# Residual by DMA transposes, a stored instruction order, and shorter runs for the k and v loads in a retention + gMLP kernel

## The chip, the cores and the metric

The kernel runs on one core of one Trainium2 chip. The metric is the device time of one execution in microseconds (us), as the median of several executions. The profile is one execution recorded by the hardware profiler. Its span (first to last instruction) is some 2 us shorter than the time. PE is the matrix engine, PEld its weight loads, DVE the vector engine, ACT the scalar engine, POOL the general engine, and SP the engine that issues nearly all DMAs here ("SPq" in a chain is SP's queue, busy with issuing).

Executions come in states: "slow" when an execution is more than 1.5% above the fastest of the same kernel. The medians in the tables are over all executions, so where one of them was slow, a difference is given here by the means of the fast ones. A ratio is the mean time of one kernel's fast runs over that of the kernel before's fast runs of the same rounds on the same chip, so it isn't quite the ratio of the medians that are quoted.

## The reference, cut to what matters

```python
# q, k, v: [8, 8, 576, 64] float32: batch, heads, sequence, head size
scores = scale * (q @ k.T)                       # per head
ret    = scores * where(rel >= 0, gamma ** rel, 0)
x      = (ret @ v) -> [8, 576, 512]              # heads side by side
h      = gelu(x @ w_in);  u, v = halves of h     # w_in: 512 x 1024
v_n    = layernorm(v) * g_ln
v_s    = einsum('ts,bsd->btd', w_sg, v_n) + b_sg # 576 x 576, along the sequence
out    = x + (u * v_s) @ w_out                   # x is the residual
```

## The kernel before

Two batches make a pair, and a pair has nine tiles of 128 rows of x. It is loaded as four full blocks (256 rows of the sequence of q, k and v) and one half block in the middle, so there are 20 blocks in 4 pairs. Every piece of work is a job with an engine, an estimated length and a due time. A planner inside the kernel simulates the engines and greedily picks the order of the jobs. Jobs on PE come in two tilings: matmuls on the whole 128x128 array (V, U, gate W, output) and 64-row ones on parts of the array (transposes T of q and k, scores S, state Z, retention output O).

```python
    # a load of a full block: one DMA each for q, k, v; runs of two rows = 512 B
    nc.sync.dma_start(f_[:], src[2*p+e, :, r0:r0+256, :].rearrange("h (p s) d -> p h (s d)", s=2))
    ...
    def a_T(b):                      # transposes of q and k: 64x64 each, four parts of the array
        for a in (1, 0):
            for kk in range(KK):
                for s in range(ns):
                    for r in range(2):
                        for c in range(2):
                            nc.tensor.transpose(tpf[C, r, o:o+64], qkb[R, s, a, 2*kk+c, :], ident[R, R])
    ...
    def a_OS(b, g):                  # O, then scores of the next block, drain, then the rest of O
        a_O(b, st.pop((b, "zs")))
        a_S(b + 1, g)
        nc.tensor.drain()
        a_O2(b)
    ...
    def m_O(i):                      # an output tile: residual by identity matmuls, then the product
        for j in range(KK):
            nc.tensor.matmul(o6[...], xTs[p][:, j, r], ident[:]..., start=(j == 0), stop=False)
        for c in range(KK):
            nc.tensor.matmul(op[:], gTs[p][:, c, r], w_out[:, c, :], start=False, stop=(c == KK - 1))
    def m_Oev(i):
        nc.scalar.activation(cur["ob", i][:], cur.pop(("op", i))[:], Act.Copy)
```

Of the kernel before, what the change touches and what calls it, by code (L numbers as in the profile page):

```python
# [19 lines left out]
SWITCH = 95.0  # L20

PR = dict(PB=10200.0, S=4803.0, S2=1401.0, OS=3150.0, Z=1500.0, Z2=2500.0, V=19148.0, V2=2200.0, U=1100.0, W=4554.0, WS=37977.0, slack=129.0, pen=766.0)
# [7 lines left out]
class Job:  # L30
    def __init__(self, eng, dur, due, fn, deps=(), new=None, uses=(), mode=None, nbytes=0, run=0, what=""):
        self.what = what or fn.__code__.co_names[:1]
        self.eng, self.dur, self.due, self.fn = eng, dur, due, fn
        self.deps = [d for d in deps if d is not None]
        self.new = [] if new is None else list(new) if isinstance(new, (list, tuple)) else [new]
        self.mode, self.nbytes, self.run = mode, nbytes, run
        self.start = self.out = None
        self.after = 0.0
        for b in uses:
            b.users.append(self)  # L40
        for b in self.new:
            b.users.append(self)


class Planner:


    def __init__(self, bufs, free, slack=60.0, penalty=500.0, fill=None, fill_until=0.0):
        self.bufs, self.free = bufs, free
        self.slack, self.penalty = slack, penalty  # L50
        self.fill, self.fill_until = fill, fill_until
        self.jobs, self.order = [], {t: [] for t in bufs}
        self.dma_free, self.dmas = 0.0, []
        self.mode = None
# [6 lines left out]
    def ready(self, j):  # L61
        t = self.free[j.eng]
        for d in j.deps:
# [3 lines left out]
            if d.eng == j.eng:  # L67
                lat = j.after if j.eng == "PE" else 60.0
# [13 lines left out]
        if j.eng == "SP" and len(self.dmas) >= 8:  # L82
            t = max(t, self.dmas[-8])
        if j.mode is not None and self.mode is not None and j.mode != self.mode:
            t += SWITCH
        return t

    def place(self, j, t):
        j.start = t
        if j.nbytes:  # L90
            self.free[j.eng] = t + j.dur
            per = (8.0 + 0.0325 * j.run) * j.nbytes / j.run / 16.0
            self.dma_free = max(self.dma_free, t + 1300.0) + per + 100.0
            j.out = self.dma_free + 700.0
            self.dmas.append(j.out)
        else:
            j.out = t + j.dur
            self.free[j.eng] = t + j.dur - OVL[j.eng]
# [4 lines left out]

    def plan(self):
        todo = {e: [] for e in self.free}
# [3 lines left out]
        while any(todo.values()):  # L109
# [15 lines left out]
            if e == "PE" and self.fill and self.free["PE"] < self.fill_until and t0 > self.free["PE"] + 500.0:  # L125
                f = self.fill(int((t0 - self.free["PE"] - 150.0) // 216.0))
# [5 lines left out]
            lim = t0 + self.slack + (SWITCH if e == "PE" else 0.0)  # L132
# [6 lines left out]
        seq = sorted(range(len(done)), key=lambda n: (done[n].start, n))  # L139
        for n in seq:  # L140
            done[n].fn()
        return max(j.out for j in done)


@with_exitstack
def kernel(
# [31 lines left out]
    BUFS = dict(ld=9, qkb=2, vb=3, qkT=2, ret=4, zb=4, xT=2, uT=2, gT=2, vg=3, mv=3, vn=10, ob=3,  # L178
# [14 lines left out]
    NBK = len(RB)  # L193

# [3 lines left out]
    g_col = consts.tile([128, KK], F32, name="g_col")  # L198
    rowg = consts.tile([4, F2], F32, name="rowg")
    rowb = consts.tile([4, S], F32, name="rowb")  # L200
    row4b = consts.tile([4, 2, S], BF, name="row4b")
    row_t = consts.tile([4, F2], F32, name="row_t")
    sel_i = consts.tile([4, 1], I32, name="sel_i")
    sel = consts.tile([4, 3], F32, name="sel")
    warm = consts.tile([128, 512], BF, name="warm")
# [5 lines left out]
    garg = consts.tile([128, 2, NBK * 2, H], F32, name="garg")  # L211
    gqv = consts.tile([128, 2, NBK * 2, H], F32, name="gqv")
# [4 lines left out]
    nc.scalar.dma_start(rowg[:], moe_g_ln.partition_broadcast(4))  # L217
    nc.scalar.dma_start(rowb[:], moe_b_sg.partition_broadcast(4))
    nc.scalar.dma_start(g_col[:], moe_g_ln.rearrange("(c p) -> p c", p=128))
# [6 lines left out]
    make_identity(nc, ident[:])  # L226
    for h in range(H):
        nc.vector.tensor_scalar(garg[:, 0, :, h], srow[:].rearrange("p n s -> p (n s)"), lng[h], lsc,
                                op0=Alu.mult, op1=Alu.add)
    nc.vector.tensor_scalar(garg[:, 1, :, :], garg[:, 0, :, :], -1.0, lsc, op0=Alu.mult, op1=Alu.add)  # L230
    nc.scalar.activation(gqv[:].rearrange("p a m h -> p (a m h)"), garg[:].rearrange("p a m h -> p (a m h)"), Act.Exp)
# [9 lines left out]
    nc.gpsimd.iota(sel_i[:], pattern=[[0, 1]], base=0, channel_multiplier=1)  # L241
    def fill(n):
        bf = Buf("d")

        def f():
            scr = psD.tile([128, 512], F32, name="scr", tag="d")
            for _ in range(n):
                nc.tensor.matmul(scr[:], warm[:, :128], warm[:], start=True, stop=True, skip_group_check=True)  # L248
        return Job("PE", 216.0 * n, 0.0, f, new=bf, mode="F")

    pl = Planner(BUFS, dict(PE=700.0, DVE=2600.0, ACT=2600.0, POOL=2600.0, SP=0.0), slack=PR["slack"], penalty=PR["pen"],
# [3 lines left out]
    HB = [PB, PB, PB / 2, PB, PB]  # L255
    T0 = []
    t = 9000.0
    for n in range(NP * NBK):
        T0.append(t)
        t += HB[n % NBK]  # L260


    wst, jw = {}, {}

    def win_load(half, c):
        bf = Buf("ld")

        def f():
            wst[half, c] = new("ld", [128, 2, F2], F32)
            w4 = moe_w_in.rearrange("(a c h d) f -> a c d h f", a=2, c=2, h=2)  # L270
            for cc in range(2):
                nc.sync.dma_start(wst[half, c][64 * cc:64 * cc + 64],
                                  w4[c, cc, :, :, half * F2:(half + 1) * F2])
        jl = add("SP", 1000.0, 0.0, f, new=bf, nbytes=1 << 19, run=2048)
        eng = "DVE" if c == 0 else "ACT"

        def g():
            src, dst = wst.pop((half, c)), w_in[:, 2 * c:2 * c + 2, half * F2:(half + 1) * F2]
            if eng == "DVE":
                nc.vector.tensor_copy(dst, src[:])  # L280
            else:
                nc.scalar.activation(dst, src[:], Act.Copy)
        jc = add(eng, 690.0 if eng == "DVE" else 1020.0, 0.0, g, deps=[jl], uses=[bf])
        jw[half, c] = jc
        return jl, jc

    def sg_load(j):
        bf, n, k_ = Buf("ld"), min(128, S - 128 * j), ("sg", j)

        def f():  # L290
            wst[k_] = new("ld", [128, S], F32)
            nc.sync.dma_start(wst[k_][:n], moe_w_sg[128 * j:128 * j + n, :])

        def g():
            nc.scalar.activation(wnat[:n, j, 64:64 + S], wst.pop(k_)[:n], Act.Copy)
        jl = add("SP", 500.0, 0.0, f, new=bf, nbytes=n * S * 4, run=2304)
        jc = add("ACT", 645.0, 0.0, g, deps=[jl], uses=[bf])
        return jl, jc

    def wo_load(c):  # L300
        bf, k_ = Buf("ld"), ("wo", c)

        def f():
            wst[k_] = new("ld", [128, 2, F2], F32)
            nc.sync.dma_start(wst[k_][:], moe_w_out.rearrange("(c p) f -> p c f", p=128)[:, c:c + 2, :])
        jl = add("SP", 500.0, 0.0, f, new=bf, nbytes=1 << 19, run=2048)
        js = []
        for r in range(2):
            def g(r=r):
                nc.scalar.mul(w_out[:, c + r, :], wst[k_][:, r, :], g_col[:, c + r:c + r + 1])  # L310
            js.append(add("ACT", 700.0, 0.0, g, deps=[jl], uses=[bf]))
        return jl, js
# [4 lines left out]
    xTs, uTs, gTs = {}, {}, {}  # L317
    cur = {}

    def a_load(b, t):  # L320
# [5 lines left out]
        if ns == 2:  # L326
            e, r0 = ch[0]
            nc.sync.dma_start(f_[:], src[2 * p + e, :, r0:r0 + 256, :].rearrange("h (p s) d -> p h (s d)", s=2))
# [4 lines left out]
    def a_prep(b, t):  # L333
# [3 lines left out]
        src = f_[:, :, :ns * D].rearrange("p h (s d) -> p s h d", s=ns)  # L337
        if t in "qk" and (b, "qkb") not in st:
            st[b, "qkb"] = new("qkb", [128, 2, 2, H, D], BF)
        if t == "k":  # L340
            nc.gpsimd.tensor_copy(st[b, "qkb"][:, :ns, 1], src)  # L341
            return
        if t == "v":
            st[b, "vb"] = new("vb", [128, 2, H, D], BF)
            dst = st[b, "vb"][:, :ns]
        else:
            dst = st[b, "qkb"][:, :ns, 0]
        a = 0 if t == "q" else 1
        for s in range(ns):
            nc.gpsimd.tensor_tensor(dst[:, s], src[:, s],  # L350
                                    gqv[:, a, 2 * n + s, :].unsqueeze(2).to_broadcast([128, H, D]), op=Alu.mult)

    def a_T(b):
# [5 lines left out]
        qkb = st[b, "qkb"]  # L359
        for a in (1, 0):  # L360
            for kk in range(KK):
                for s in range(ns):
                    o = ((a * KK + kk) * ns + s) * 64
                    for r in range(2):
                        for c in range(2):
                            R, C = slice(64 * r, 64 * r + 64), slice(64 * c, 64 * c + 64)
                            nc.tensor.transpose(tpf[C, r, o:o + 64], qkb[R, s, a, 2 * kk + c, :], ident[R, R])  # L367

    def a_Tev(b):
        ns = RB[b % NBK][0]  # L370
        w = 2 * KK * ns * 64
        nc.vector.tensor_copy(st[b, "qkT"][:].rearrange("p c a k t -> p c (a k t)")[:, :, :w],  # L372
                              st.pop((b, "tp"))[:].rearrange("p c a k s t -> p c (a k s t)")[:, :, :w])
# [502 lines left out]
```

## Time and profile before

| | kernel before |
|---|---|
| time, median | 241.68 us (240.2 to 243.03, 3 runs); with the run beside the changed kernel 240.94 us (238.7 to 243.03, 4 runs) |
| span of the profiled run | 239.6 us |
| PE busy | 215.4 us, 90% |
| DVE, ACT, POOL busy | 57%, 56%, 53% |
| time in DMA packets, mean of the 16 DMA engines | 155.3 us |
| transposes of block 5 start on PE | 60.68 us |
| first gate matmul on PE | 61.32 us |
| last matmul starts | 235.4 us |

The lines themselves stand in the prediction below. The page is read from the top: who is busy, then when (the slices), then what the end waited for (the chain), then which group of instructions that is. A high busy share alone doesn't bound the time. The chain does, because it is followed back from the last instruction.

### The profile page before, as it was taken

Reading aid. Unit: us, or ns where it says so; the run is one execution under the profiler, and the core shown is the slowest. Engines: PE = TensorE matmul, PEld = TensorE weight load, DVE = VectorE, ACT = ScalarE, POOL = GpSimd, SP = SyncE. Lnnn points to the kernel's source line nnn. Section 1 sums busy time; section 2 is a strip of 40 time slices with the busy share of each in tenths; the row PEclk is TensorE's granted clock in tenths of the full one; section 3 lists DMA queues with packets and bytes.
Section 4 is the critical chain, followed back from the end, with each engine's and each line's share of the span. In section 5 each row is a group of like instructions: output and inputs, shape, how many; then the busy total and the mean of one; then the engine's idle time right before and its main releaser. Section 6 shows DMA issues by size and latency. Waiting matters only on the chain.

```text
span 239.6 us, 10051 instructions
## 1 busy us (share of the span) xinstructions
PE 215.4 (90%) x4440; PEld 148.0 (62%) x4485; DVE 137.1 (57%) x230; ACT 135.1 (56%) x234; POOL 126.8 (53%) x198
## 2 busy tenths in 40 slices
PE   7975839887989999999999999899999999999993
PEld 2442617654766676677676667566757666667761
DVE  7991626665765745665667466374756555634420
ACT  2027247865656475576645665767473656865422
POOL 8955645499595569772437497906083802221000
PEclk9999989999999999999999999999999999999998
DMA  6999589999899985898564658971110220111324
GB/s 177 251 237 259 138 260 328 290 277 267 176 302 280 310 219 149 244 294 238 149 196 137 193 140 253 298 198 47 48 47 11 80 94 34 59 47 44 131 92 175
DMA packets 70765, 42.92 MB, mean 179 GB/s; under 512 B 14817, under 2 KB 63993, under 8 KB 70721
## 3 DMA queue, kind: packets, MB, share of 16 engines
q1 hardware_dynamic: 70176, 42.26, 63.4%
q8 instruction: 35, 0.57, 1.1%
q10 hardware_dynamic: 544, 0.02, 0.2%
q14 instruction: 10, 0.07, 0.1%
HBM read 32.80 MB, written 9.44 MB: 176 GB/s over the span
## 4 chain that ended last, share of the span: by engine, by line
PE 76%; DMA 13%; issue 4%; ACT 3%; SPq 1%; POOL 1%; ACTq 0%
PE wp L575 17%; PE hu L559 13%; PE op L596 13%; PE hv L517 12%; PE pp L439 7%; DMA ld<-in_q_dram 4%; PE pp L367 4%; PE pp L393 4%; PE op L593 3%; DMA ld<-in_moe_w_out_dram 3%; DMA ld<-in_moe_w_in_dram 3%; PE zp L421 3%; DMA ld<-in_moe_w_sg_dram 2%; ACT xT L506 1%; PE scr L248 1%
## 5 line engine op out<-in xcount | busy, mean ns | idle before, releaser
L403 DVE TENSOR_TENSOR ret<-pp,msk 128x1024 bf16<-128x1024 f32 x32 | 38.9, 1220 | 27.8 <-PE pp L393 27.6
L350 POOL TENSOR_TENSOR qkb<-ld,gqv 128x512 bf16<-128x512 f32 x36 | 37.1, 1051 | 15.6 <-DMA ld<-in_q_dram 12.9
L350 POOL TENSOR_TENSOR vb<-ld,gqv 128x512 bf16<-128x512 f32 x36 | 38.2, 1081 | 5.8 <-DMA ld<-in_v_dram 3.6
L575 PE MATMUL wp<-wT,vn 128*128 128x288 bf16 x256 | 41.2, 286 | 0.0
L582 DVE TENSOR_TENSOR gT<-wp,uT 128x288 bf16<-128x288 f32 x64 | 28.7, 453 | 21.0 <-PE wp L575 20.8
L533 POOL TENSOR_SCALAR mv<-mv 128x2 f32<-128x2 f32 (+1 forms) x20 | 4.5, 226 | 67.5 <-DVE mv L529 48.9
L559 PEld LDWEIGHTS <-w_in 128*128 128x128 bf16 x576 | 34.4, 98 | 6.9 <-issue 0.3
L559 PE MATMUL hu<-xT,w_in 128*128 128x128 bf16 x576 | 38.3, 219 | 0.2 <-issue 0.2
L517 PE MATMUL hv<-w_in,xT 128*128 128x512 bf16 x122 | 35.6, 380 | 2.6 <-ACT xT L506 1.4
L528 DVE BATCH_NORM_STATS2 bst<-vg 128x6 f32<-128x512 f32 x36 | 24.8, 690 | 19.3 <-ACT vg L521 19.3
L596 PE MATMUL op<-w_out,gT 128*128 128x512 bf16 x127 | 33.4, 379 | 0.9
L521 ACT ACTIVATE vg<-hv 128x512 f32<-128x512 f32 x36 | 21.5, 596 | 20.3 <-PE hv L517 18.1
L600 ACT ACTIVATE ob<-op 128x512 f32<-128x512 f32 x36 | 21.4, 595 | 19.4 <-PE op L596 19.4
L372 DVE COPY qkT<-pp 128x2048 bf16<-128x2048 bf16 (+1 forms) x20 | 22.2, 1111 | 15.1 <-PE pp L367 15.1
L565 ACT ACTIVATE uT<-hu 128x512 bf16<-128x512 f32 x36 | 21.5, 596 | 15.6 <-PE hu L559 15.6
L548 ACT ACTIVATE vn<-vg,mv 128x512 bf16<-128x512 f32 x32 | 25.0, 809 | 8.8 <-POOL mv L536 8.7
L506 ACT ACTIVATE xT<-pp 128x512 bf16<-128x512 f32 (+1 forms) x40 | 24.6, 665 | 8.2 <-PE pp L439 8.2
L575 PEld LDWEIGHTS <-vn 128*128 128x128 bf16 x256 | 23.9, 98 | 6.7
L517 PEld LDWEIGHTS <-xT 128*128 128x128 bf16 x144 | 12.6, 98 | 13.1 <-ACT xT L506 2.4
L341 POOL CAST qkb<-ld 128x1024 bf16<-128x1024 f32 (+1 forms) x20 | 19.5, 975 | 0.5 <-DMA ld<-in_k_dram 0.5
L248 PE MATMUL scr<-warm 128*128 128x512 bf16 x61 | 17.6, 436 | 2.2 <-DVE warm L221 1.2
L421 PE MATMUL zp<-vb,qkb 64*64 64x64 bf16 x480 | 13.8, 194 | 6.1 <-ACT zb L427 4.4
(66 smaller groups left out, 263.9 us busy)
## 6 DMA issues: line engine op xcount, KB each, us to landing
out_dram<-ob SPq DMA_DIRECT2D x36, 256.0 KB, 2.7
ld<-in_q_dram SPq DMA_DIRECT2D x16, 512.0 KB, 5.5
ld<-in_k_dram SPq DMA_DIRECT2D x16, 512.0 KB, 6.9
ld<-in_v_dram SPq DMA_DIRECT2D x16, 512.0 KB, 8.1
ld<-in_moe_w_in_dram SPq DMA_DIRECT2D x8, 256.0 KB, 7.0
ld<-in_moe_w_sg_dram SPq DMA_DIRECT2D x4, 288.0 KB
ld<-in_q_dram SPq DMA_DIRECT2D x8, 128.0 KB, 5.1
ld<-in_k_dram SPq DMA_DIRECT2D x8, 128.0 KB, 3.6
```

The lines of the kernel that those rows point to most:

```text
L350: nc.gpsimd.tensor_tensor(dst[:, s], src[:, s], gqv[:, a, 2 * n + s, :].unsqueeze(2).to_broadcast([128, H, D]), op=Alu.mult)
L372: nc.vector.tensor_copy(st[b, "qkT"][:].rearrange("p c a k t -> p c (a k t)")[:, :, :w], st.pop((b, "tp"))[:].rearrange("p c a k s t -> p ...
L403: nc.vector.tensor_tensor(ret[:].rearrange("p r (k t) -> p (r k) t", k=2), sc[:].rearrange("p r (k t) -> p (r k) t", k=2), msk2[:].rearran ...
L506: nc.scalar.activation(dst, src, Act.Copy)
L517: nc.tensor.matmul(hv[:], xTs[p][:, kk, 128 * m:128 * m + 128], w_in[:, kk, F2:], start=(kk == 0), stop=(kk == KK - 1))
L521: nc.scalar.activation(vgs[i][:], cur.pop(("hv", i))[:], Act.Gelu_apprx_tanh)
L528: nc.vector.bn_stats(bst[:], vgs[i][:])
L548: nc.scalar.activation(vn[:], vg[:], Act.Identity, scale=mv[:, s, 2:3], bias=mv[:, s, 3:4])
L559: nc.tensor.matmul(hu[:, c, :], w_in[:, kk, 128 * c:128 * c + 128], xTs[p][:, kk, 128 * m:128 * m + 128], start=(kk == 0), stop=(kk == KK ...
L575: nc.tensor.matmul(ps[:], vns[t0 + j][e][:, 128 * c:128 * c + 128], wT[e][j][:, half * HS:(half + 1) * HS], start=(j == 0), stop=(j == SB ...
L582: nc.vector.tensor_tensor(gTs[p][:, c, col:col + HS], cur.pop(("wp", b, c, half))[:], uTs[p][:, c, col:col + HS], op=Alu.mult)
L596: nc.tensor.matmul(op[:], gTs[p][:, c, r], w_out[:, c, :], start=False, stop=(c == KK - 1), skip_group_check=True)
```

## The change

The intent is to take work and waits off PE, and to bring the start forward. The parts:

- The residual of pairs 1 to 3 leaves PE: a DMA transposes x back into rows, and the DVE adds it as it empties the accumulator.
- The planner follows a stored order (searched for beforehand) and no longer plans greedily. Its model also counts a fetch of instructions for each 256 rows of PE, and different switches between tilings. Within PE, the drain ahead of the second part of O is replaced by another job and a semaphore.
- The q and k transposes are joined in twos (64x128), 576 instead of 1152. U jobs take two tiles, so 512 of its matmuls of 128 columns become 256 of 256.
- k and v of a full block are loaded in two DMAs of 256 B runs each. q stays in one DMA of 512 B runs. There are twelve load buffers instead of nine, weights come in fewer DMAs, the small rows for g and b are made on PE and ACT instead of by DMA copies, and block 0's q and k are prepared on DVE and ACT.

```diff
@@ a load of a full block
-            nc.sync.dma_start(f_[:], src[2 * p + e, :, r0:r0 + 256, :].rearrange("h (p s) d -> p h (s d)", s=2))
+            rows = src[2 * p + e, :, r0:r0 + 256, :].rearrange("h (p s) d -> p h s d", s=2)
+            if t == "q":
+                nc.sync.dma_start(f_[:], rows)
+            else:
+                for s in range(2):
+                    nc.sync.dma_start(f_[:, :, s * D:s * D + D], rows[:, :, s])
@@ transposes of q and k
-                        for c in range(2):
-                            nc.tensor.transpose(tpf[C, r, o:o + 64], qkb[R, s, a, 2 * kk + c, :], ident[R, R])
+                        ins = nc.tensor.transpose(tpf[:, r, o:o + 64], qkb[R, a, kk, s].rearrange("p c d -> p (c d)"), ident[R, R])
@@ the second part of O
-            a_S(b + 1, g)
-            nc.tensor.drain()
+        on = pend.pop(b)
+        if on is None:
+            nc.tensor.drain()
+        elif on:
+            nc.tensor.wait_ge(swap, on)      # an early matmul of the job in between has counted it up
@@ the output
+    XP = 1
+        if p < XP:                           # identity matmuls for pair 0 alone
...
+    def m_X(i):
+        cur["xr", i] = new("xr", [128, KK, 128], BF)
+        nc.sync.dma_start_transpose(cur["xr", i][:], xTs[p][:, m].rearrange("p j r -> p (j r)"))
     def m_Oev(i):
+        if i // NT < XP:
+            ins = nc.scalar.activation(ob[:], op[:], Act.Copy)
+        else:
+            ins = nc.vector.tensor_tensor(ob[:], op[:], cur.pop(("xr", i))[:].rearrange("p j r -> p (j r)"), op=Alu.add)
@@ the order
+ORDER = ( '0 f9 1 6 81 2 111 83 7 f11 ...' )    # 34 lines; job numbers, fN is filler matmuls
     def plan(self):
+        if ORDER:
+            return self.follow(ORDER)
... (joined weight loads, rows of g and b, gate written over u, fused POOL work: cut)
```

## The prediction

> **What bounds the kernel now.** I read the page from the top: busy time per engine, then the slices.
>
> ```profile
> PE 215.4 (90%) x4440; PEld 148.0 (62%) x4485; DVE 137.1 (57%) x230; ACT 135.1 (56%) x234; POOL 126.8 (53%) x198
> ## 2 busy tenths in 40 slices
> PE   7975839887989999999999999899999999999993
> ...
> PEclk9999989999999999999999999999999999999998
> DMA  6999589999899985898564658971110220111324
> ```
>
> The reader is to see two stages. From slice 11 (60 us) to slice 38 the matrix engine (PE) is 90% busy or more at full clock, while DMA runs dry after slice 28. In the first ten slices PE has holes and DMA is at eight or nine tenths: the start waits for loads. A busy PE may still be a slow PE, so the next view is the chain that ended last.
>
> ```profile
> PE 76%; DMA 13%; issue 4%; ACT 3%; SPq 1%; POOL 1%; ACTq 0%
> PE wp L575 17%; PE hu L559 13%; PE op L596 13%; PE hv L517 12%; PE pp L439 7%; DMA ld<-in_q_dram 4%; PE pp L367 4%; PE pp L393 4%; PE op L593 3%; DMA ld<-in_moe_w_out_dram 3%; DMA ld<-in_moe_w_in_dram 3%; PE zp L421 3%; DMA ld<-in_moe_w_sg_dram 2%; ACT xT L506 1%; PE scr L248 1%
> ```
>
> The path is matmuls, with 13% of DMA, all of it before 45 us when the chain is read in order of time. The stage table confirms it (columns: us, busy us of PE, weight loads, DVE, ACT, POOL, then clock, DMA share, GB/s):
>
> ```profile
> 0.00:20.00 20.00, 17.22 (x219) 8.26 (x223) 16.93 (x31) 4.62 (x7) 14.07 (x31) 1.00 0.99 230
> 20.00:40.00 20.00, 12.35 (x307) 8.63 (x309) 7.91 (x14) 10.90 (x19) 11.06 (x14) 0.91 0.89 230
> 40.00:60.00 20.00, 16.61 (x427) 11.75 (x430) 12.53 (x21) 12.37 (x23) 15.69 (x22) 1.00 1.03 286
> 60.00:110.00 50.00, 47.61 (x1151) 34.19 (x1159) 31.00 (x50) 31.61 (x57) 34.44 (x49) 1.00 0.94 249
> 110.00:160.00 50.00, 47.51 (x1078) 33.48 (x1086) 29.83 (x48) 30.68 (x55) 29.44 (x43) 1.00 0.71 202
> 160.00:203.00 43.00, 41.79 (x937) 29.63 (x947) 25.11 (x43) 25.66 (x46) 18.14 (x29) 1.00 0.13 46
> ```
>
> In the chain in order of time the same U job (16 matmuls) of successive pairs of batches starts at 129.80 and 180.62: one pair takes 50.8 us. Steady savings must come out of that period. The groups that matter:
>
> ```profile
> L559 PE MATMUL hu<-xT,w_in 128*128 128x128 bf16 x576 | 38.3, 219 | 0.2 <-issue 0.2
> L593 PE MATMUL op<-ident,xT 128*128 128x128 bf16 x144 | 13.9, 219 | 0.0
> L582 DVE TENSOR_TENSOR gT<-wp,uT 128x288 bf16<-128x288 f32 x64 | 28.7, 453 | 21.0 <-PE wp L575 20.8
> L403 DVE TENSOR_TENSOR ret<-pp,msk 128x1024 bf16<-128x1024 f32 x32 | 38.9, 1220 | 27.8 <-PE pp L393 27.6
> L367 PE MATMUL pp<-ident,qkb 64*64 64x64 bf16 x1152 | 13.5, 194 | 3.4 <-POOL qkb L341 2.2 <-issue 1.1
> ```
>
> The 219 ns of L559 is latency; start to start the 16 matmuls of a job take 0.89 us, 56 ns each. Costs on PE below are start to start, from the timeline.
>
> [...] 56 ns at 128, 216 ns at 512 columns. [...] going from 128x128 matmuls to 64x64 ones costs 0.093 us beyond streaming, back 0.12 us. [...] 256 B packets took 19.4 ns in the mean (12288 of them), 512 B packets 30.7 ns (49152), so half the bytes cost 63% of the time. [...]
>
> **The change part by part.**
>
> Residual. In pairs 1 to 3 the four identity matmuls (L593) ahead of each output job go: 27 jobs x 4 x 56 ns = 6.1 us of PE, all in the saturated stage, so all on the path. In exchange there are 27 DMA transposes of 128 KB, and 27 output evacuations go from ACT (595 ns) to DVE, as an add. From 453 ns at 288 elements and 1220 ns at 1024, a PSUM read on DVE costs 153 + 1.042 n ns, so 0.69 us at 512: 18.5 us more DVE, 16.1 us less ACT. DVE in a steady pair: 31.0 us per 50 now; plus 9 x 0.69 in a shorter 47 us gives about 36, or 77%. It stays under PE. A transpose at ordinary packet cost is an estimated 512 x 19.4 / 16 = 0.6 us of the engines, 17 us in all, where DMA has room.
>
> U jobs. 512 of the 576 matmuls become 256 of 256 columns: a pair of tiles from 2 x 16 x 55.8 = 1786 ns to 16 x 109.2 = 1747 ns. Sixteen pairs: 0.6 us.
>
> Drains. Before the second part of O the old kernel drains PE after the S job. In the PE timeline the first matmul after it starts 0.32 to 0.34 us after the last of S (15 times between 60 and 203 us). The new order puts another job between and waits for a semaphore of an early matmul of it. I count 18 x 0.30 = 5.4 us.
>
> Order. In the instruction order the switches between large and 64-row jobs fall from 53 to 41 each way: 12 x (0.093 + 0.12) = 2.6 us less. But the q/k transposes, halved from 1152 to 576 of 64x128 tiles, are now a third tiling: borders between them and the other small jobs go from 16 to 30, each now a switch. At some 0.1 us each (my choice, from the other switches) that gives back 3.0 us. Streaming stays: 32 matmuls on two tiles against 64 on four.
>
> Instruction fetch. PE rows fall from 8972 to 6990, mostly from transposes and U. Between 60 and 203 us five stalls inside small-matmul jobs, right behind a 16 KB instruction packet, cost 3.4 us; one of 1.43 us comes earlier. I count 2 us saved.
>
> Steady sum: 6.1 + 0.6 + 5.4 + 2.6 - 3.0 + 2.0 = 13.7 us.
>
> Start. Moving k and v in 256 B runs turns 32768 packets into 65536: (65536 x 19.4 - 32768 x 30.7) / 16 = 16.6 us more of each engine over the whole run, and about 6.4 us in the first five blocks (10 loads of 512 KB x 0.52, and a rest for block five). Against it, weights load in fewer DMAs, the small row copies through DMA vanish, w_out moves behind block five's q and k, and twelve buffers instead of nine let loads run ahead. Before, block 4's transposes start at 50.7 us, though its loads sum to 38.6 us of packets, some 43 us with start and landing: 7 us were lost to queue waits. After: q 7.9, k and v 17.4, half block 3.7, w_in 6.2, w_sg 4.0, sum 39.2, landed at 43.5, transposes at 45; block 5 at about 54.5. Up to block 5's transposes PE had done some 28 us of work by 60.7 us (32.7 lost); by the new order it will have done 30 us by 54.5 (24.5 lost). That is 8 us if the queue never waits; I take 6.
>
> Total 13.7 + 6 = 19.7, so 241.7 - 19.7 = 222 us. The old tail of 4 us stays.
>
> **The rivals.** A: the loads decide. Every full block costs 7 us of DMA instead of 5.9, and PE waits longer for blocks 4 to 6. For it: DMA share is near 1 up to 80 us. Against: after the weights a block needs 7 us and PE about 11 (50.8 / 4.5). If the start gains nothing: 228 us; if it loses 4 us: 232. B: the transposes become the new wait. They stand in the same queue as loads of up to 512 KB, behind stores that wait for their data (the queue's waits for ACT ob were 89 us), with three buffers; a late one holds DVE, which now also frees the score and gate buffers in order. At 0.3 us per output: 8 us back, 230 us. For it: DVE at 77%. Against: DMA shares of 0.71 and 0.13 in that stage. C: the order fits better than I count, few waits left and cheap transposes: 15 us steady plus 9 at the start plus the 3 us of the third tiling, 214 us.
>
> **Range and chances.** Residual and drains are firm, 11.5 us; taken alone they are nearly 5%. Start and waits spread by 8 us each way, more upwards. Prediction 222 us, range 213 to 231. Faster by over 2% means below 236.8: 0.95; within 2%: 0.04; slower: 0.01.
>
> **What would show it.** Right: no identity group beyond 36 matmuls; PE period per pair near 47.5 us; block 5's transposes near 54 us; the gap ahead of O's second part under 0.1 us; 256 B packets near 77800 at about 19 ns; DVE add near 0.69 us and DVE near 150 us. Wrong: PE idle after 60 us released by DVE or by a transpose (B), PE holes before 70 us released by k or v loads (A), or borders of the transposes far from 0.1 us. A period above 49 us would refute the steady sum; first gate matmuls after 58 us would refute the start.

In the trace of the kernel before, from 62 us on, matmuls of 128 columns start every 55.9 ns in the mean, and those of 512 columns every 216 ns (median). The 55.8 and 109.2 ns of the U term (128 and 256 columns) were calculated; for 256 columns a straight line through 56 and 216 ns gives 109.3 as an estimate, and the changed kernel's trace has 109.6 in the mean. That a transpose costs ordinary packets was the assumption; the kernel before has no transpose, and the changed kernel's took 21.4 ns a packet. "Streaming stays" was an expectation: a T job takes 0.71 us on the timeline of the kernel before (64 matmuls from 60.68 us) and 0.64 joined (32 from 67.42 us).

## The result

The changed kernel takes 227.26 us (226.66 to 229.07, 4 runs), against 240.94 us of the kernel before in the same rounds. The ratio is 0.9484 (95% interval 0.9404 to 0.9564). The result is correct and the profiled run is a fast one. So it is faster by over 2%, as predicted, inside the range, and 5.3 us above the predicted 222 us.

Busy time per engine and three rows of the slices, of the changed kernel:

```profile
PE 205.5 (91%) x3514; PEld 138.0 (61%) x3514; DVE 147.8 (66%) x266; ACT 123.3 (55%) x214; POOL 114.2 (51%) x157
## 2 busy tenths in 40 slices
PE   7987599793999999999999689999999999999991
PEclk9999979998599999999999999999999999999999
DMA  6999999989999998989999999999896154344664
```

PE lost ten us of work, but its share of the span hardly rose. DMA is now at eight or nine tenths almost without a break up to slice 30, where before it was at four to six tenths in slices 20 to 24 and ran dry from slice 28 on. And PE has holes where before it had none: slice 10 (3 tenths, with the clock at half in slice 11), and slice 23. The chain that ended last says the same:

```profile
PE 64%; DMA 14%; SPq 8%; POOL 5%; DVE 3%; issue 2%; ACT 1%; POOLq 0%; DVEq 0%
```

It was 76% PE before. DMA transfers, their issue and the POOL work behind them now make 27% of the path. In stages (columns: window, us, then busy us of PE, weight loads, DVE, ACT, POOL, then clock, DMA share, GB/s):

```profile
20.00:40.00 20.00, 16.78 (x351) 11.54 (x345) 12.12 (x22) 15.81 (x30) 13.52 (x18) 0.91 1.10 270
40.00:60.00 20.00, 14.94 (x281) 10.83 (x274) 10.34 (x19) 10.72 (x20) 12.51 (x13) 0.87 0.95 229
60.00:110.00 50.00, 50.00 (x954) 34.87 (x953) 31.03 (x51) 33.58 (x60) 31.92 (x38) 0.99 1.02 232
110.00:160.00 50.00, 47.02 (x919) 31.97 (x918) 36.50 (x59) 28.67 (x52) 31.49 (x41) 1.00 1.15 224
160.00:203.00 43.00, 42.79 (x685) 28.70 (x683) 32.04 (x57) 21.76 (x38) 15.62 (x24) 1.00 0.56 122
```

The DMA share from 60 to 160 us rose from 0.94 and 0.71 to 1.02 and 1.15. (The share is summed from the packets' own times, which overlap a little, so it passes 1 here.) At the holes, the timeline of PE reads (start, us, engine, line, operation, count, and in brackets the idle time before it and what ended it):

```profile
51.02 0.62 PE L586 MATMUL pp<-ret,vb 64*64 64x128 bf16 x32
55.12 1.03 PE L501 MATMUL pp<-ident,qkb 64*128 64x64 bf16 x32 [3.48 <-POOL qkb L455]
...
56.87 1.14 PE L719 MATMUL wp<-wT,vn 128*128 128x288 bf16 x4
...
125.00 0.64 PE L501 MATMUL pp<-ident,qkb 64*128 64x64 bf16 x32 [0.74 <-POOL qkb L455]
126.85 0.44 PE L565 MATMUL zp<-vb,qkb 64*64 64x64 bf16 x16 [1.22 <-POOL vb L461]
```

L455 is POOL's cast of k, which itself waits for the load of k. In the chain, the k load issued at 48.02 us is on the path for 5.88 us, then POOL, then these transposes of block 5. After the idle 3.48 us PE runs at half clock: 15 gate matmuls take 3.71 us of the chain, where ones at full clock take 1.84. The clock's records have half clock from 54.63 to 61.46 us. The clock falls 3.0 us into the gap; in e8 below it is at half behind gaps of 2.75 and 2.40 us as well. So in this execution one late load cost PE twice: the wait, and about 2.9 us at half clock (worked out under e1 below). The fourth execution was granted a clock of 0.991 where this one had 0.977, and it took 227.78 us all the same. So the loss doesn't need the half clock.

Two groups (columns: line, engine, operation, tiles, shapes, count, busy us, mean ns, idle before):

```profile
L762 DVE TENSOR_TENSOR ob<-op,xr 128x512 f32<-128x512 f32 x27 | 18.5, 690 | 8.6 <-PE op L746 8.4
L741 PE MATMUL op<-ident,xT 128*128 128x128 bf16 x36 | 3.5, 219 | 0.0
```

The residual moved as intended: 36 identity matmuls are left of 144, and 27 adds on the DVE take 690 ns each.

### The profile page after: what moved, and what is told of

Same layout as the page of the kernel before. It is cut to its first block, busy times and chain, and to the rows that moved or that the text cites. A ratio compares the mean times of both kernels' runs of the same rounds, so it can differ in the third digit from the quotient of the medians.

```text
span 225.0 us, 8170 instructions
## 1 busy us (share of the span) xinstructions
PE 205.5 (91%) x3514; PEld 138.0 (61%) x3514; DVE 147.8 (66%) x266; ACT 123.3 (55%) x214; POOL 114.2 (51%) x157
## 4 chain that ended last, share of the span: by engine, by line
PE 64%; DMA 14%; SPq 8%; POOL 5%; DVE 3%; issue 2%; ACT 1%; POOLq 0%; DVEq 0%
PE wp L719 16%; PE op L746 12%; PE hu L700 11%; PE hv L653 11%; DMA ld<-in_k_dram 5%; SPq L433 5%; PE pp L586 5%; PE pp L501 3%; PE pp L533 3%; DMA ld<-in_v_dram 2%; PE zp L565 2%; DMA ld<-in_q_dram 2%; DMA wst<-in_moe_w_sg_dram 2%; POOL vb L461 2%; SPq L436 2%
## 5 line engine op out<-in xcount | busy, mean ns | idle before, releaser
L461 POOL TENSOR_TENSOR qkb<-ld,gqv 128x1024 bf16<-128x1024 f32 (+1 forms) x19 | 32.7, 1723 | 24.9 <-DMA ld<-in_q_dram 8.2
L729 DVE TENSOR_TENSOR uT<-wp,uT 128x288 bf16<-128x288 f32 x64 | 28.4, 451 | 22.8 <-PE wp L719 21.5
L461 POOL TENSOR_TENSOR vb<-ld,gqv 128x1024 bf16<-128x1024 f32 (+1 forms) x20 | 34.7, 1733 | 11.2 <-DMA ld<-in_v_dram 9.4
L700 PE MATMUL hu<-xT,w_in 128*128 128x256 bf16 (+1 forms) x320 | 38.2, 266 | 1.0 <-ACT vg L660 1.0
L653 PE MATMUL hv<-w_in,xT 128*128 128x512 bf16 x144 | 37.9, 390 | 0.7 <-ACT xT L642 0.7
L746 PE MATMUL op<-w_out,uT 128*128 128x512 bf16 x144 | 35.8, 380 | 0.0
L700 PEld LDWEIGHTS <-w_in 128*128 128x128 bf16 x320 | 28.2, 99 | 8.7 <-issue 1.6
L688 ACT ACTIVATE vn<-vg,mv 128x512 bf16<-128x512 f32 x32 | 25.1, 810 | 10.7 <-POOL mv L676 10.6
L660 ACT ACTIVATE vg<-hv 128x512 f32<-128x512 f32 x36 | 21.4, 595 | 15.1 <-PE hv L653 8.3
L762 DVE TENSOR_TENSOR ob<-op,xr 128x512 f32<-128x512 f32 x27 | 18.5, 690 | 8.6 <-PE op L746 8.4
L455 POOL CAST qkb<-ld 128x1024 bf16<-128x1024 f32 (+1 forms) x19 | 18.0, 947 | 11.3 <-DMA ld<-in_k_dram 11.3
L574 ACT ACTIVATE zb<-zp 128x256 bf16<-128x256 f32 x32 | 12.2, 381 | 16.0 <-PE zp L565 15.9
L746 PEld LDWEIGHTS <-uT 128*128 128x128 bf16 x144 | 13.0, 98 | 12.3 <-DVE uT L729 0.4
```

Source lines behind the costliest of these rows:

```text
L461: eng.tensor_tensor(dst, src, g.unsqueeze(3).to_broadcast(list(src.shape)), op=Alu.mult)
L653: ins = nc.tensor.matmul(hv[:], xTs[p][:, m, kk, :], w_in[:, kk, F2:], start=(kk == 0), stop=(kk == KK - 1))
L660: unfence(nc.scalar.activation(vgs[i][:], cur.pop(("hv", i))[:], Act.Gelu_apprx_tanh), ("V", i))
L688: nc.scalar.activation(vn[:], vg[:], Act.Identity, scale=mv[:, s, 2:3], bias=mv[:, s, 3:4])
L700: ins = nc.tensor.matmul(hu[:, n, :], w_in[:, kk, 128 * c:128 * c + 128], xTs[p][:, m:m + w, kk, :], start=(kk == 0), stop=(kk == KK - 1), ...
L729: ins = nc.vector.tensor_tensor(uTs[p][:, c, col:col + HS], cur.pop(("wp", b, c, half))[:], uTs[p][:, c, col:col + HS], op=Alu.mult)
```

## The experiments

All twelve kernels gave correct results. The time of the kernel before in the three sets was 240.96, 239.42 and 240.54 us. "The changed kernel with 512 B runs" below means the first experiment's.

| run | kernel | time, us (range) | ratio to before (95%) |
|---|---|---|---|
| | changed kernel | 227.26 (226.66 to 229.07) | 0.9484 (0.9404 to 0.9564) |
| e1_runs512 | changed, k and v in one DMA of 512 B runs | 214.68 (213.87 to 215.26) | 0.8935 (0.8861 to 0.9008) |
| e2_greedy | changed, stored order emptied | 256.00 (254.78 to 257.03) | 1.0655 (1.0562 to 1.0748) |
| e3_resid_pe | changed, residual on PE | 230.07 (228.77 to 233.72) | 0.9560 (0.9464 to 0.9655) |
| e4_drain | changed, with drains | 231.31 (229.96 to 234.40) | 0.9624 (0.9476 to 0.9772) |
| e5_before256 | before, k and v in 256 B runs | 252.80 (251.84 to 253.15) | 1.0559 (1.0517 to 1.0602) |
| e6_two512 | changed, two DMAs, 512 B runs | 213.56 (212.70 to 214.09) | 0.8920 (0.8875 to 0.8964) |
| e7_512_pe | e1, residual on PE | 219.43 (218.75 to 219.97, and one of 515.22) | 0.9161 (0.9116 to 0.9207) |
| e8_512_t64 | e1, 64x64 transposes | 228.32 (225.10 to 233.58) | 0.9468 (0.9382 to 0.9553) |
| e9_512_greedy | e1, stored order emptied | 241.56 (241.03 to 242.08) | 1.0101 (1.0022 to 1.0180) |
| e11_512_shift64 | e1, 64 empty rows ahead on PE | 214.78 (213.86 to 216.24) | 0.8977 (0.8923 to 0.9031) |
| e12_two512_tail | e6, last two residuals on PE | 213.66 (212.55 to 214.23) | 0.8922 (0.8871 to 0.8974) |
| e13_512_drain | e1, with drains | 218.53 (217.42 to 220.47) | 0.9136 (0.9077 to 0.9196) |

### The loads: four runs

The theory was that the 256 B runs of k and v are a loss that the rest of the change pays for. The rival was that the two DMAs let the work on k and v start earlier, or at least cost nothing.

e1_runs512:

```diff
-            if t == "q":
+            if t in "qkv":
                 nc.sync.dma_start(f_[:], rows)
```

> Undoes one part alone: k and v again one DMA a block with runs of 512 bytes; every engine's order is as in the changed kernel. Theory (the loads in 256 B runs are what the gain was lost to): 32768 packets of 30.8 ns in place of 65536 of 21.4 ns free 24.6 us of each DMA engine; the wait for block 5's k (PE idle 3.5 us before 55 us, then half clock, some 3 us) and the PE holes of 112 to 128 us (3.5 us) shrink or go: 218 to 221 us, and the DMA share falls well below 0.9. Rival (the order was made for these loads, or their time is hidden beside PE): within 1% of 227 us.

Measured: 214.68 us, 12.6 us less than the changed kernel, more than expected. The chain that ended last is now nearly all PE:

```profile
PE 88%; issue 3%; DMA 3%; DVE 2%; SPq 1%; DVEq 0%; POOL 0%; ACTq 0%; POOLq 0%
```

The PE order is the same in both, so their times can be compared job by job. The transposes of block 5 start at 49.70 us against 55.12 (5.4 us). Those of block 6 start at 59.08 against 67.42 (8.3 us), and between the two lies the half clock. From there to block 12 nothing more is lost (112.21 against 120.55, again 8.3 us). Block 14's start at 126.86 against 138.48 (11.6 us). So 5.4 us are lost in the start, 2.9 to the half clock behind the hole, and 3.3 between 121 and 139 us, where the waits for k and v shown above lie. The stages of this run:

```profile
40.00:60.00 20.00, 19.84 (x425) 14.21 (x424) 15.04 (x27) 14.66 (x27) 16.74 (x16) 1.00 1.02 266
60.00:110.00 50.00, 49.43 (x962) 35.65 (x966) 33.05 (x53) 34.99 (x63) 32.15 (x42) 1.00 1.05 270
110.00:160.00 50.00, 49.42 (x950) 34.33 (x958) 37.94 (x64) 31.52 (x56) 34.42 (x43) 1.00 0.93 196
```

PE has no hole in the stretch from 40 to 60 us and runs at full clock there, and DMA's share falls under 1 from 110 us.

e6_two512 keeps two DMAs but gives each four heads in 512 B runs:

```diff
-                    nc.sync.dma_start(f_[:, :, s * D:s * D + D], rows[:, :, s])
+                    nc.sync.dma_start(f_[:, 4 * s:4 * s + 4, :], rows[:, 4 * s:4 * s + 4])
```

> The changed kernel with k and v in two DMAs a block still, but each of four heads with 512 B runs. It tells the size of the packets from the number of DMAs. Packet size is the cost: 214 to 217 us, as with one DMA of 512 B runs (214.7). Number of DMAs is the cost (32 more issues of some 0.7 to 1.4 us on the queue's engine): 222 to 227 us.

(The issue time expected there compares with the changed kernel's trace: issuing one k or v load kept SP busy for a median of 0.96 us.)

Measured: 213.56 us, ratio 0.892 against 0.8935 of e1, just below the range expected if the packet size is the cost. The number of DMAs costs nothing that can be seen. The packet size is the whole cost, within that.

e5_before256 puts the same loads alone into the kernel before:

```diff
-            nc.sync.dma_start(f_[:], src[2 * p + e, :, r0:r0 + 256, :].rearrange("h (p s) d -> p h (s d)", s=2))
+            rows = src[2 * p + e, :, r0:r0 + 256, :].rearrange("h (p s) d -> p h s d", s=2)
+            if t == "q":
+                nc.sync.dma_start(f_[:], rows)
+            else:
+                for s in range(2):
+                    nc.sync.dma_start(f_[:, :, s * D:s * D + D], rows[:, :, s])
```

> The kernel before with one part of the change alone: k and v of a full block in two DMAs of 256 B runs, nothing else. Theory (the runs cost engine time, 16.6 us of each engine over the run by the packet records, and the kernel before has slack for only a part of it): the start loses 5 to 6 us and the stretch from 60 to 110 us, at a DMA share of 0.94, a few more: 246 to 254 us, with k and v loads as releasers. Rival (the 12.6 us that they cost in the changed kernel come from its order, which has no slack for them): 240 to 244 us.

Measured: 252.80 us, 13.4 us over the kernel before in the same rounds, at the upper end of the theory; the rival falls. The cost doesn't hang on the new order. But the theory named k and v loads as what PE would wait for, and the largest wait isn't one of them. The largest piece is one hole of PE in the timeline, which the kernel before doesn't have:

```profile
100.12 1.04 PE L522 MATMUL hv<-w_in,xT 128*128 128x512 bf16 x4
107.34 1.87 PE L564 MATMUL hu<-xT,w_in 128*128 128x128 bf16 x16 [6.18 <-ACT ob L605]
```

PE waits for an accumulator that ACT is to empty into an output buffer. That the output buffer was not free because its store stands in the same queue behind the loads is my reading of this line. No run took it apart.

The sizes, from the packet records. 256 B packets took 21.4 ns in the mean in the changed kernel and 512 B packets 30.8 ns. The time in packets per DMA engine was 155.3 us before and 174.0 with the 256 B runs alone. It was 206.6 in the changed kernel and 185.1 with 512 B runs. So the shorter runs cost 18.7 and 21.5 us of every DMA engine. Up to 60 us the four kernels are alike, at 58.4, 57.7, 62.1 and 61.8 us: the engines have no room there, and what is added can only come later.

### The order: two runs

e2_greedy and e9_512_greedy empty the stored order, so that the kernel's own greedy planner runs, with its new model and its new jobs:

```diff
-ORDER = ( '0 f9 1 6 81 2 111 ...' )
+ORDER = ""
```

> Undoes the annealed order alone: the stored order is emptied, so the planner's own greedy choice orders all jobs; all jobs, transposes and loads are as in the changed kernel. If the stored order carries the steady saving (fewer switches, no waits for buffers): 233 to 238 us, with more switches of tiling and PE idle. If the saving comes from the jobs alone (residual off PE, no drains): within 1.5% of 227 us.

Measured: 256.00 us, 28.7 us more than the changed kernel and more than the kernel before. That is outside both expectations.

> The changed kernel with 512 B runs for k and v and the stored order emptied, so that the kernel's own greedy planner orders the jobs. Theory (the order itself is the largest part of the gain, whatever the loads: it was searched over a model that counts waits for buffers, switches and one instruction fetch per 256 rows of PE): 236 to 246 us, with PE busy below 88%. Rival (the greedy order lost 28.7 us with the 256 B runs because it has no slack for these loads): 222 to 230 us.

Measured: 241.56 us, 26.9 us more than e1. The theory holds (PE is busy 88%, at the edge of what it said): against this greedy order, the stored one is worth the same with either loads. The chain of e9:

```profile
PE 60%; DVE 11%; ACT 8%; DMA 5%; POOL 5%; SPq 4%; issue 4%; ACTq 0%; POOLq 0%; DVEq 0%
```

DVE, ACT and POOL stand on the path with 24%, where in e1 PE has 88% of it. With this greedy order, all other parts of the change together bring nothing over the kernel before, which was greedy too. (The greedy planner's due times are those stored beside the order. Whether another set would do better was not tried, so how much of the 27 us is the order and how much a planner with unsuited settings is not shown.) All other runs keep the stored order, which was made for the changed kernel's own jobs. So what they put back is measured in an order that may not suit it.

### The residual: two runs

e3_resid_pe and e7_512_pe put the residual of all pairs back on PE:

```diff
-    XP = 1
+    XP = 4
...
+                        if p >= 1:
+                            add("SP", 0.0, due - 6000.0, lambda: None)   # keeps the numbers of the stored order
```

> Undoes the transposes alone: the residual of all pairs by identity matmuls on PE and evacuated by ACT, in the same order. Theory of the prediction: PE gets 27 x 4 x 56 ns = 6.1 us back, so about 232 to 233 us if nothing waits for transposes. Rival (transposes took 17 us of full DMA engines and held the loads, and the last ones hold the end by 1 us): 227 to 230 us, since the loads' waits shrink by what the transposes took.

Measured: 230.07 us. Its three fast executions have a mean of 229.6 us against 227.6 of the changed kernel, 2.1 us more, and the intervals of the two ratios overlap. The theory's 232 to 233 us fails, the rival's range holds. Its profile fell in a slow execution, so no times are read from it.

> The changed kernel with 512 B runs for k and v, and the residual of all pairs on PE by identity matmuls, as in the kernel before. Without the 256 B runs PE is at 99% from 60 to 195 us, so 27 x 4 matmuls of 56 ns should count in full: 214.7 + 6.1 = 220 to 221 us, less up to 1 us of a shorter tail. Rival (transposes give back about half on the DMA queue whatever the loads, as the 2.8 us with 256 B runs suggest): 216.5 to 218 us.

Measured: 219.2 us in the mean of the three fast executions, 4.6 us more than e1, and 5.7 more than e6, which ran in the same rounds. That lies between the two expectations, nearer to the first. Taking 6.1 us off PE saves some 4.6 to 5.7 us where DMA has some room (a share of 0.93 from 110 to 160 us in e1) and about 2 where it has none (1.15 in the changed kernel). (One of the four executions, the profiled one, took 515.22 us. The median in the table still counts it; see the last section.)

### The drains: two runs

e4_drain and e13_512_drain put a drain ahead of the wait:

```diff
         elif on:
+            nc.tensor.drain()
             nc.tensor.wait_ge(swap, on)
```

> Puts one suspected saving back: a drain of PE before the second part of each O job, all else as in the changed kernel. The prediction counted 18 x 0.30 = 5.4 us for the drains' going. If they cost that: 231 to 233 us. If a drain there is mostly hidden by the switches and semaphore waits that stand there anyway: 227 to 229 us.

Measured: 231.31 us. One of the four executions was slow; the fast ones are 3.3 us above the changed kernel in the mean, with intervals that overlap.

> The changed kernel with 512 B runs for k and v, and a drain of PE ahead of every second part of O, in addition to the semaphore. Prediction's term: 18 x 0.30 = 5.4 us, 220 us. With the 256 B runs it was 4.05 us; if the loads hid a part of it there, 219.5 to 220.5 us here. Rival (a drain behind another job than S costs less than the 0.3 us seen before, and 4 us is its whole worth): 218 to 219.2 us.

Measured: 218.53 us, 3.85 us more than e1, and 3.75 more than e11, which turned out to be a repeat of e1 (see below), in the same rounds. The rival holds: 4 us is the whole worth. In the PE timeline the first matmul behind a drain starts 0.26 to 0.30 us late, as before the change. Without a drain that gap isn't zero everywhere: about 0.02 us behind a Z job but 0.105 us behind joined transposes, because that border is now a switch of tiling (in e8 below, where it is none, the gap is 0.006 us).

### The joined transposes and the instruction fetch: two runs

e8_512_t64 undoes the joining:

```diff
-                        ins = nc.tensor.transpose(tpf[:, r, o:o + 64], qkb[R, a, kk, s].rearrange("p c d -> p (c d)"), ident[R, R])
+                        for c in range(2):
+                            ins = nc.tensor.transpose(tpf[64 * c:64 * c + 64, r, o:o + 64], qkb[R, a, kk, s, c], ident[R, R])
```

> The changed kernel with 512 B runs for k and v, and the q and k transposes as 1152 of 64x64 in place of 576 of 64x128. Theory of the prediction (the joined form is a third tiling, 30 more borders at some 0.1 us = 3.0 us, while the streaming is the same): 64x64 saves 3 us and loses 1 to 2 us to the fetch of 1150 more PE rows: 212.5 to 214.5 us. Rival (the joined form pays for itself by fewer rows and fewer fetch stalls): 216 to 218 us.

Measured: 228.32 us. Its two fast executions have a mean of 226.5 us, some 12 us above e1: the wrong way for the theory and far beyond the rival. The borders did get cheaper (O to T 0.014 us instead of 0.13, T to O 0.006 instead of 0.105). But PE stops at places where it waits for nothing that the profile shows:

```profile
50.24 0.72 PE L502 MATMUL pp<-ident,qkb 64*64 64x64 bf16 x64
...
54.56 0.37 PE L587 MATMUL pp<-qkT,zb 64*64 64x128 bf16 x5 [3.55 <-issue]
...
92.28 0.43 PE L587 MATMUL pp<-qkT,zb 64*64 64x128 bf16 x8 [2.75 <-issue]
...
173.69 0.40 PE L720 MATMUL wp<-wT,vn 128*128 128x288 bf16 x1 [2.40 <-issue]
```

Inside each of these three stops a packet of 16 KB of the instruction queue starts (at 52.00, 89.60 and 171.33 us, taking 1.0 to 1.2 us each). The run has 32 such packets against 27 in e1. The traces' counts go together with PE's rows: the kernel before has 4440 matmuls and 4485 weight loads and 35 such packets, 255 rows a packet; the changed kernel has 3514 of each and 27, 260 rows a packet; e8 has 4090 of each and 32, 256 rows a packet. From these I estimate some 256 rows of PE a packet. And each of the three stops shows the same sign in the records: the next instruction packet starts 3.5 to 3.9 us after the first, and between the two PE started only 24, 12 and 6 weight loads, where 4090 / 32 = 128 is the run's mean between two packets. My reading is that PE had used up what was fetched; no record shows that directly. All three come within 3 us behind a T job. A full T job now has 128 rows, weight loads and transposes, in 0.72 us on the timeline; the joined form has 64 rows in 0.64. After 30 us, gaps of PE of over 1 us sum to 11.1 us in this run, and e1 has none. Each of the three stops also brings half clock (6.83 us from 53.97, 6.83 from 91.52 and 3.41 from 173.44). The profile fell in a slow execution (233.58 us at a clock of 0.962), so this overstates the fast runs, and only the kind of stop is taken from it. The fast execution of 225.10 us had a clock of 0.992, no lower than e1's 0.990, and was still over 10 us slower, so the half clock isn't the main part.

e11_512_shift64 asks whether the stored order depends on where the borders between these packets fall:

```diff
+    for _ in range(64):
+        nc.tensor.nop(nofuse=True)
```

> The changed kernel with 512 B runs for k and v, and 64 rows that do nothing ahead of everything on PE, where PE waits for the first memset anyway. [...] Theory (the stored order puts the fetch borders where PE has other waits or slow rows, and this is why 64x64 transposes, which shift all borders and shorten the time of 256 rows, lost 13.6 us): 216 to 220 us, with stalls of over 0.9 us in other places than in the run with 512 B runs alone. Rival (borders do not matter, only the number of rows does): 213.5 to 215 us.

Measured: 214.78 us against 214.68. But this run is void as a test. That the empty rows would shift all later ones was taken for granted in the expectation. Counting the weight loads that PE had started at each instruction packet gives the same places in both runs (1798 and 1799, 2149 and 2149, 3418 and 3418 at the fourteenth, seventeenth and last packet). A shift of 64 rows, half of them weight loads, would have moved these by 32. So these counts show no shift, the run is a repeat of e1, and all that it shows is that e1's median repeats within 0.1 us. (The ratios to the kernel before, 0.8935 and 0.8977, differ by 1 us, so comparisons between sets of rounds are good to about that.)

So two readings stay open. Either the joined form helps because the dense 64-row jobs have fewer rows, or the stored order was fitted to the places of the fetches and any shift would cost. That PE ran out of instructions in e8 is what its slow profile points to; whether this makes up the 12 us of the fast runs, and which of the two makes the joined form free of it, is not shown.

### A last version

e12_two512_tail takes e6 and has the last two output tiles add their residual on PE:

```diff
+    PEX = set(range(NT)) | {N - 2, N - 1}
-        if p < XP:
+        if i in PEX:
```

> A version that should beat all others: two DMAs of four heads with 512 B runs for k and v, and the last two output tiles with their residual on PE and their evacuation on ACT, as pair 0 has it, so that the end does not wait for the last two transposes (the last DVE adds waited 1.5 us for them with 512 B runs). Theory: PE gains 8 matmuls of 56 ns = 0.45 us, the end loses 1.5 us of waiting: 212 to 213 us against 213.6. Rival (the last store and not the transposes sets the end): 213.5 to 214.5 us.

Measured: 213.66 us against 213.56 of e6. No gain; the time is in the rival's range. In the profiled runs the tail after the last matmul's start did get shorter, from 5.1 to 4.1 us; in the medians this isn't seen. That the last store sets the end is argued, not shown. The best version is the changed kernel with 512 B runs for k and v, in one DMA or two: 11% faster than the kernel before.

## Why the prediction was right or wrong

The class and the range were right. The point was 5.3 us too low, and the parts were further off than the sum. Cut at block 5's transposes, the start saved 5.6 us (60.68 to 55.12; 6 were predicted) and the rest of the span 9.0 us (178.9 to 169.9; 13.7 predicted). In e1 the same cut gives 11.0 and 15.0 us. So the missing part is in the steady sum, and it is missing because of the loads. That the total stayed in the range is in part luck: the 256 B runs cost 12.6 us, of which the sum had 6.4, while the order and the joined transposes brought more than was counted.

**Residual, 6.1 us.** The mechanism was right (36 identity matmuls left, 690 ns per add as worked out, DVE at 147.8 us against the 150 predicted). The size was about 2 us in the kernel as it is and 4.6 to 5.7 us with 512 B runs. The prediction gave the transposes "room" on the DMA engines; that was the mis-sized term. The packets alone say so: 27 x 512 packets x 21.4 ns (the mean of all 256 B packets) / 16 = 18.5 us of each engine. With the transposes taken out, the sum of all packet times falls by more, from 206.6 to 174.5 us in e3 and from 185.1 to 155.2 in e7 (both profiles are of slow executions). The rest is in the other packets, which took longer beside them: those of 4 B took 10 ns in the mean without transposes and 35 and 43 ns with them.

**U jobs, 0.6 us.** Eight matmuls of 256 columns take 0.87 us in the chain, 109 ns each, as predicted. No run tested the term by itself.

**Drains, 5.4 us.** They measured about 3.3 and 3.85 us. The 0.3 us per drain was right. What was missed is that the gap doesn't vanish behind joined transposes (0.105 us). The check "under 0.1 us" held behind Z and failed there.

**Order, 2.6 us, third tiling, -3.0 us, and instruction fetch, 2.0 us.** This was the weakest part. Counting switches gave 2.6 us for the order; emptying it cost 27 to 29. That is not a like for like measure of the old order, but the greedy planner was the old way too. The borders of the third tiling were sized well (0.105 to 0.133 us each). But the joined form as a whole was counted as a loss of 3 us and a part of the 2 us of fetch, while undoing it cost some 12 us. The step that failed is "I count 2 us saved": it added up stalls that the old kernel had, where the question was how many the new order would have without the joining. That these 12 us are fetch stalls is likely from e8's profile and not shown. (PE's rows fell to 7028 and not to 6990.)

**Start, 6 us.** The checks came out well: transposes of block 5 at 55.12 us (predicted "near 54"), first gate matmul at 47.72 (before 58). The estimate of 6.4 us for the 256 B runs up to block 5 is met by 5.4 us in e1. What was missed is the hole itself, 3.48 us behind a load of k, and the half clock after it. The hole is the prediction's own sign that rival A is right ("PE holes before 70 us released by k or v loads").

**Rival A, the loads decide.** It gave 228 us if the start gains nothing, and the result was 227.26. The start did gain, but PE did wait for k and v there and later, as A has it. The argument against A was the step of the prediction that failed: "after the weights a block needs 7 us and PE about 11". It counted loads alone. With the measured packets, a full block needs (1024 x 30.8 + 4096 x 21.4) / 16 ns = 7.4 us for loads. Two output stores take 2 x 128 x 101.3 / 16 = 1.6 us, and two transposes 2 x 512 x 21.4 / 16 = 1.4 us. That makes 10.4 us. PE needed 47.5 us per pair by the prediction's own period, which is 47.5 / 4.5 = 10.6 us per block. There is hardly any slack left. The first transpose is issued at 107.88 us; before it the sum is 9.0 us, and from block 6 to block 12 PE lost nothing against e1. The waits of 121 to 131 us come after it. With 512 B runs the sum with transposes is about 9.0 us, and there PE is busy 99% of the time from 60 to 160 us.

**Rival B, transposes as a wait.** As a wait of the DVE it is hardly seen: the last transpose stands in the chain at the end (3.22 us from 217.14), and in e1 the DVE waited for one 1.5 us there. What the transposes cost, they cost as packets beside the loads. **Rival C, 214 us, all better.** It was wrong for this kernel. That e1 takes 214.68 us is coincidence, since C was not about its loads.

**Tail, "4 us stays".** PE's last matmul starts at 220.0 us and the span is 225.0, so the tail is about 1 us longer than before.

**Packets.** The prediction expected 77800 packets of 256 B at 19 ns. There were 91649 at 21.4 ns: 13824 are the transposes', which the prediction priced but left out of this count.

**The period of 47.5 us.** This check was ill chosen. The stored order shifts work between pairs: the U job of the middle tile, one per pair, starts at 36.33, 95.55, 134.01 and 182.99 us, distances of 59.2, 38.5 and 49.0 us. A single distance neither proves nor refutes the steady sum. Even in the kernel before, the chosen job's starts are 80.62, 129.80 and 180.62 us, so 49.2 and then 50.8 us, and the prediction took the larger.

**Readings.** Three small slips changed nothing: slices 12 and 26 of PE are at 8 tenths and not at 9; DMA runs dry from slice 28 on and not after it; and DVE in a pair is 31.0 x 50.8 / 50 + 6.2 = 37.7 us, or 79% of 47.5, and not 36 and 77% (36.5 of 50 us were measured from 110 to 160 us).

## What to carry to other kernels

Before counting a transfer as hidden, add up all that the DMA engines have to move in one period of the compute engine (loads, stores and what the change itself adds), each at the packet time that the trace shows, and compare with the period. When several changes come together, undo each alone: here one of them cost 12.6 us that the others paid for, and the version without it runs at 215 instead of 227 us. In a kernel in which five engines hand work to each other, the order of the work can be worth more than the instructions saved: here emptying the stored order cost 26.9 us (with the caveat on the greedy planner's settings above), and putting the residual's matmuls back on PE 4.6 to 5.7.

## Also measured

- Instruction fetch: the 16 KB packets took 1.20 us in the mean in the kernel before (35) and 1.23 in the changed kernel (27). PE stopped for 2.40 to 3.55 us around three of them in e8_512_t64, each time with two packets 3.5 to 3.9 us apart and PE almost still between them. How much PE holds of what was fetched is not shown.
- Half clock: the records show it behind PE gaps of 3.48 us in the changed kernel, 4.07 in the kernel before (half clock from 33.57 us) and 3.55, 2.75 and 2.40 in e8_512_t64. The changed kernel's stretch from 27.33 us begins 2.4 us after the end of a gap of 2.82 us. A gap of 2.22 us in the kernel before (up to 23.98 us) brought none. Each whole stretch of half clock in these three profiles lasted 3.41 or 6.83 us.
- Transposes: in the changed kernel 8192 packets of 256 B behind the last load, which are 16 of the transposes, took 21.4 ns in the mean, and those before the first transpose 20.5. SP was busy 1.19 to 2.3 us with issuing one transpose of 128 KB, and it landed 2.4 to 6.9 us later, median 3.2. The mean 4 B packet took 10 ns in the kernel before and 35 in the changed kernel.
- Switches of tiling: 0.093 us from 128x128 to 64x64, 0.12 to 0.135 back, and 0.105 to 0.133 between 64x64 and 64x128.
- One execution of e7_512_pe took 515.22 us, with gate matmuls of 570 ns in the mean instead of 287 (e1's) and PE busy 99%, while the records of the granted clock gave 1.00 throughout. The same kernel took 218.75 to 219.97 us in its other three executions. What slowed it is open.
